# A new written order for a one-core kernel of linear attention and a highway layer: how x is turned, where the last columns are cut, and what fills TensorE at the start

## The chip, the core and the metric

The kernel runs on one core of a Trainium2 chip. A core has five engines with a queue each: TensorE (PE, matrix products, results in eight banks of PSUM), VectorE (DVE), ScalarE (ACT), GpSimd (POOL) and SyncE (SP, here the engine that issues nearly all DMA transfers). Each works through its own instructions in order and waits on semaphores for the others. The metric is the device time of one execution in microseconds (us), the median over several runs. Lower is better.

## The reference

The inputs are q, k and v of shape 4 x 8 x 768 x 64 (batch, heads, positions, head dimension), a decay `lam` per head, and a highway layer with two 512 x 512 matrices and a bias.

```python
for b in range(nb):                       # 12 blocks of 64 positions
    intra = einsum('bhic,bhjc->bhij', qb, kb) * Dmask      # Dmask[i,j] = lam**(i-j), i >= j
    intra = einsum('bhij,bhjd->bhid', intra, vb)
    inter = einsum('bhid,bhde->bhie', qb * lam_pow, kv_state)
    out[:, :, sl] = intra + inter
    kv_state = lam_block * kv_state + einsum('bhsd,bhse->bhde', kb * rev_pow, vb)
x = out.transpose(0, 2, 1, 3).reshape(3072, 512)
H = maximum(x @ w_h, 0);  T = sigmoid(x @ w_t + b_t)
return T * H + (1 - T) * x
```

## The kernel before

The work is cut into 12 steps n = 0 to 11: three for each of the four batches, of 256 positions each. A step holds two tiles b = 0, 1 of 128 positions, all eight heads in it, and the highway layer runs on the same tile of 128 x 512. Instead of a state that is scaled in each block, q is multiplied by lam to the position and v by its inverse, so that the state of a batch is a plain sum in PSUM (the bank `pair`, seen as `kv`).

The order in which everything is issued stands in a string, `PLAN`. It is a list of tokens that is executed from the left. Each token names an action, a step, mostly a tile or half, after `@` the engine and after `=` the PSUM banks (0 to 6). The compiler does not reorder, so each engine's queue is the sequence of its tokens. The tokens:

- `Lq`, `Lk`, `Lv` load half a step of q, k or v (256 KB each) on SyncE, or on ScalarE's queue with `@ACT`. `W` loads half of a weight matrix, `WC` casts a quarter of it to bf16.
- `CQ`, `CK`, `CV` make bf16 of q (times its power), k, and v (times its power); the last number is the half, 2 means both at once. `CQ` and `CV` run mostly on POOL.
- `TQ`, `TK` turn q and k on TensorE by products with the identity: in the form with a last number 0 in 64-row pieces (32 for both together), with 1 whole (16 for both). `EB` copies the result out of PSUM.
- `S`, and `SP` with the state sums `U` woven in, are the score products; `M` multiplies them by the mask on DVE; `KE` copies the state out; `I` are the products with the state, `A` those of the masked scores with v (the value products). `D` copies the finished x, which is turned (position along the free axis), to `xT`.
- `XT` turns x back on TensorE and `XE` copies it to `xr`. `XD` does the same by a DMA transpose from SyncE, without TensorE and without a copy. `xr` has three buffers, `xT` six.
- `PB` presets a bank with the bias, `F.n.b.w` multiplies the tile with a weight matrix (w = 0 for h, 1 for the gate t), `H` is relu minus x on DVE, `G` the sigmoid in place on ACT, `X` the product of both on DVE, `AD` the final sum (POOL mostly), `ST` the store. A further number p takes only the columns 256 p to 256 p + 255 of 512.
- `Z` are idle products: r times identity times zeros into a bank, which nothing reads. `ZT` does one into each bank, at the very start. `B` makes the bias row into 128 rows.

The loads have five buffers for each of q, k and v, the transfers eight completion semaphores, which the issues take in turn: an issue waits until the one eight places ahead has landed. Functions that matter: `turn` and `evac_x` (L375 to L393 of the kernel before), `block` (L405), `small` (L412), `spin` (L453), `open_banks` (L457).

Of the kernel before, what the change touches and what calls it, by code (L numbers as in the profile page):

```python
# [22 lines left out]
I.1.1=0 I.1.0=4 SP.1.1=6 CK.2.2@POOL D.0.1@ACT D.0.0@ACT M.1.0.0@DVE M.1.0.1@DVE W.1.0 TK.2.1=35 W.1.1 KE.1.1@ACT
WC.0.0.1@ACT WC.0.0.0@DVE Lq.3.1 Lq.3.0 WC.0.1.1@DVE WC.0.1.0@ACT CQ.2.2@POOL XT.0=2 A.1.1 A.1.0 D.1.1@DVE TQ.2.1
D.1.0@ACT F.0.0.0=6 XE.0@DVE EB.2.0@ACT XT.1=0 F.1.1.0=2 CV.2.2@POOL WC.1.1.0@POOL EB.2.1@DVE XE.1@DVE PB.0.1@ACT=4
WC.1.0.1@ACT PB.0.0@ACT=1 H.1.1@DVE WC.1.0.0@ACT F.0.1.0=5 F.1.0.0=0 H.0.0@DVE SP.2.0=362 H.0.1@DVE H.1.0@DVE Lk.3.0
Lk.3.1 M.2.1.1@DVE M.2.1.0@DVE M.2.0.0@DVE WC.1.1.1@ACT F.0.1.1 KE.2.0@ACT PB.1.1@ACT=0 G.0.1@ACT F.0.0.1 I.2.1=3
I.2.0=6 X.0.1@DVE SP.2.1=2 F.1.1.1 M.2.0.1@DVE CQ.3.2@POOL Lv.3.0 PB.1.0@ACT=5 AD.0.1@POOL TQ.3.0=24 Lv.3.1 G.0.0@ACT
CK.3.2@ACT Lq.4.0 Lq.4.1 TK.3.0 CV.3.2@POOL CQ.4.2@POOL X.0.0@DVE A.2.1 A.2.0 EB.3.1@ACT EB.3.0@DVE D.2.1@DVE
G.1.1@ACT D.2.0@ACT F.1.0.1 X.1.1@DVE SP.3.0=426 G.1.0@ACT KE.3.0@ACT Lk.4.0 Lk.4.1 Lv.4.0 XT.2=0 Lv.4.1 I.3.1=3  # L30
M.3.0.0@DVE M.3.1.1@DVE AD.1.1@POOL XE.2@ACT CK.4.2@ACT SP.3.1=1 F.2.1.0=6 M.3.0.1@DVE CV.4.2@POOL TQ.4.0=02 Lk.5.0
Lk.5.1 Lq.5.1 Lq.5.0 A.3.1=1 M.3.1.0@DVE AD.0.0@POOL A.3.0 TK.4.0 PB.2.1@ACT=4 D.3.1@ACT H.2.1@DVE D.3.0@DVE
EB.4.1@DVE X.1.0@DVE KE.3.1@ACT EB.4.0@ACT F.2.0.0=6 AD.1.0@POOL H.2.0@DVE XT.3=1 SP.4.0=023 F.2.1.1 KE.4.0@DVE
PB.2.0@ACT=5 XE.3@ACT I.4.1=6 I.4.0=1 M.4.1.1@DVE M.4.1.0@DVE M.4.0.0@DVE SP.4.1=2 Lv.5.1 CQ.5.2@POOL Lq.6.1 Lv.5.0
Lq.6.0 Lk.6.1 Lk.6.0 F.2.0.1 M.4.0.1@DVE Lv.6.1 Lv.6.0 CV.5.2@POOL G.2.1@ACT CK.5.2@ACT TK.5.0=30 X.2.1@DVE TQ.5.0
EB.5.1@DVE A.4.1 CQ.6.2@POOL A.4.0 KE.4.1@ACT G.2.0@ACT PB.3.1@ACT=4 CV.6.2@POOL Lq.7.0 Lk.7.0 D.4.0@ACT Lq.7.1
D.4.1@ACT EB.5.0@DVE Lk.7.1 F.3.1.0=2 SP.5.0=301 H.3.1@DVE F.3.1.1 CK.6.2@ACT M.5.1.1@DVE X.2.0@DVE TK.6.1=26 Lv.7.0
# [477 lines left out]
```

## Time and profile before

| what | us |
|---|---|
| median of three runs | 102.2 (102.17 to 103.01) |
| profiled execution | 102.22 |
| its span, first to last instruction | 100.5 |
| TensorE busy | 90.9 (90%) |
| VectorE busy | 81.1 (81%) |
| GpSimd busy | 74.5 (74%) |
| ScalarE busy | 72.0 (72%) |

DMA moved 28.61 MB, 285 GB/s in the mean. A product of TensorE is shown with a modelled end, so its busy time also holds short waits between products. The chain of waits is followed back from the last instruction: each piece is the work that released the next. In the timeline, what stands in square brackets is the idle time of that engine just before and what ended it.

### The profile page before, as it was taken

The page shows a single profiled execution, that of the slowest core. Times are in us where ns is not written, and L with a number is a line of the kernel's source. Part 1 is how long each engine was busy: PE and PEld are TensorE (multiplying, and loading weights), DVE is VectorE, ACT ScalarE, POOL GpSimd, SP SyncE. Part 2 cuts the span into 40 slices and gives each one's busy share as a digit, 9 for nine tenths or more (in the row PEclk, how much of TensorE's full clock was granted, in tenths as well). Part 3 has the DMA queues.
Part 4 walks back from the last instruction along what each step waited for, and adds up shares of the span by engine and source line. Part 5 has one row for each costly group of instructions (what it writes and reads, how often), then busy time and mean ns, then how long its engine had stood idle before and what let it go on. Part 6 is the DMA issues. An engine that isn't in the chain of part 4 may idle for free.

```text
span 100.5 us, 4427 instructions
## 1 busy us (share of the span) xinstructions
PE 90.9 (90%) x1891; PEld 54.0 (54%) x1891; DVE 81.1 (81%) x143; ACT 72.0 (72%) x123; POOL 74.5 (74%) x64
## 2 busy tenths in 40 slices
PE   4988999999998999999999999999999999999400
PEld 1314455873465666657656576666555565458200
DVE  4225386999987899999999979989998969996840
ACT  2436307989679899999799999887999867563400
...
GB/s 9 234 331 366 351 362 400 373 394 352 334 266 332 358 363 306 285 298 342 313 303 294 295 305 320 324 354 316 184 312 342 147 156 52 182 251 290 373 110 108
DMA packets 41222, 28.61 MB, mean 285 GB/s; under 512 B 6129, under 2 KB 37361, under 8 KB 41202
## 3 DMA queue, kind: packets, MB, share of 16 engines
...
q10 hardware_dynamic: 418, 0.27, 0.8%
...
HBM read 20.98 MB, written 6.29 MB: 271 GB/s over the span
## 4 chain that ended last, share of the span: by engine, by line
PE 74%; DVE 9%; ACT 5%; DMA 4%; POOL 2%; issue 1%; ACTq 0%; POOLq 0%; DVEq 0%
PE pb L409 40%; PE pb L296 8%; DVE m L349 6%; PE pb L367 5%; PE pb L271 5%; PE pb L357 4%; DMA qf<-in_q_dram 4%; PE pb L455 3%; PE pb L268 2%; PE kv L301 2%; POOL qb L243 2%; PE pb L383 2%; ACT kqT L110 2%; ACT pb L422 2%; DVE gxh L425 1%; PE pb L451 1%
## 5 line engine op out<-in xcount | busy, mean ns | idle before, releaser
L409 PE MATMUL pb<-w_b,xT 128*128 128x512 bf16 (+1 forms) x208 | 46.6, 364 | 0.5 <-ACT pb L422 0.4
L349 DVE TENSOR_TENSOR m<-pb,tri 128x512 bf16<-128x512 f32 x48 | 31.0, 682 | 4.3 <-PE pb L296 4.0
L428 POOL TENSOR_TENSOR o<-gx,xr 128x512 f32<-128x512 bf16 x22 | 25.2, 1154 | 10.3 <-DVE gx L425 8.3
L243 POOL TENSOR_TENSOR qb<-qf,pow_q 128x1024 bf16<-128x1024 f32 (+1 forms) x14 | 23.7, 1693 | 5.8 <-DMA qf<-in_q_dram 5.8
L409 PEld LDWEIGHTS <-xT 128*128 128x128 bf16 x208 | 18.2, 97 | 17.3 <-issue 0.9
L250 POOL TENSOR_TENSOR vs<-vf,pow_v 128x1024 bf16<-128x1024 f32 (+1 forms) x12 | 21.2, 1772 | 3.0 <-DMA vf<-in_v_dram 3.0
L422 ACT ACTIVATE pb<-pb 128x512 f32<-128x512 f32 (+1 forms) x26 | 14.1, 552 | 5.0 <-PE pb L409 3.8
L110 ACT ACTIVATE kqT<-pb 128x1024 bf16<-128x1024 bf16 x12 | 12.2, 1024 | 6.6 <-PE pb L268 4.2
L425 DVE TENSOR_TENSOR gx<-pb,hm 128x512 bf16<-128x512 f32 x22 | 15.0, 683 | 1.0 <-ACT pb L422 0.3
L417 DVE SCALAR_TENSOR_TENSOR hm<-pb,xr 128x512 bf16<-128x512 f32 x22 | 14.7, 683 | 0.8 <-PE pb L409 0.8
L296 PE MATMUL pb<-kqT 64*64 64x128 bf16 x384 | 14.7, 220 | 0.6 <-ACT xT L110 0.3
L403 ACT ACTIVATE pb<-bt_all 128x512 f32<-128x512 f32 x24 | 14.1, 602 | 0.9 <-DVE m L349 0.5
L296 PEld LDWEIGHTS <-kqT 64*64 64x64 bf16 x384 | 11.0, 105 | 3.9 <-ACT kqT L110 1.2
L110 ACT ACTIVATE xT<-pb 128x512 bf16<-128x512 f32 x19 | 10.9, 595 | 2.7 <-PE pb L367 2.6
L301 PE MATMUL kv<-vs,kb 64*64 64x64 bf16 x320 | 11.8, 193 | 0.0
L110 ACT ACTIVATE kb<-kf 128x1024 bf16<-128x1024 f32 (+1 forms) x10 | 10.1, 1011 | 1.7 <-DMA kf<-in_k_dram 1.7
L112 DVE COPY kqT<-pb 128x1024 bf16<-128x1024 bf16 x12 | 8.1, 686 | 2.4 <-PE pb L271 2.3
L301 PEld LDWEIGHTS <-kb 64*64 64x64 bf16 x320 | 9.8, 107 | 0.4 <-issue 0.4
L110 ACT ACTIVATE ss<-kv 128x256 bf16<-128x256 f32 x17 | 6.5, 385 | 2.4 <-PE pb L296 1.6
L367 PE MATMUL pb<-m,vs 64*64 64x128 bf16 x384 | 7.7, 218 | 0.2 <-DVE m L349 0.2
L455 PE MATMUL pb<-blank,id 128*128 128x512 bf16 x26 | 7.8, 439 | 0.0
L367 PEld LDWEIGHTS <-vs 64*64 64x64 bf16 x384 | 6.0, 106 | 2.6 <-issue 2.3
...
## 6 DMA issues: line engine op xcount, KB each, us to landing
...
```

The lines of the kernel that those rows point to most:

```text
L110: A.activation(dst, src, AF.Copy)
L243: ENG[eng].tensor_tensor(new(("qb", n), [128, 4, 4, D])[:, :, ys], in0=get("qf", n)[:, ys].rearrange("p y (i d) -> p i y d", i=4), in1=pow ...
L250: ENG[eng].tensor_tensor(new(("vs", n), [128, H, J, D])[:, hs], in0=get("vf", n)[:, hs].rearrange("p h (j d) -> p h j d", j=J), in1=pow_v[ ...
L296: T.matmul(get("s", n, e, hp // 2)[half(b), hp % 2, j, :], lhsT=keys(n, e, hp, j, b), rhs=queries(n, e, hp, b), start=first("s", n, e, hp ...
L301: T.matmul(kv[half(e), hp], lhsT=get("kb", n)[half(b), j, 2 * hp + e, :], rhs=get("vs", n)[half(b), 2 * hp + e, j, :], start=fresh, stop=T ...
L349: V.tensor_tensor(new(("m", n, e, u), [128, 2, J, C]), in0=get("s", n, e, u), in1=tri[:, None].to_broadcast([128, 2, J, C]), op=ALU.mult)
L367: T.matmul(get("o", n, b)[half(e), hp, :], lhsT=get("vs", n)[half(b), 2 * hp + e, j, :], rhs=get("m", n, e, u)[half(b), hp % 2, j, :], sta ...
L409: T.matmul(t, lhsT=get("xT", n, b)[:, kc, :], rhs=w_b[w][:, kc, cs], start=(w == 0 and kc == 0), stop=(kc == KC - 1), skip_group_check=boo ...
L417: V.scalar_tensor_tensor(small("hm", n, b, p), in0=get("h", n, b, p), scalar=0.0, in1=get("xr", n)[:, b, cols(p)], op0=ALU.max, op1=ALU.su ...
L422: A.activation(t, t, AF.Sigmoid)
L425: V.tensor_tensor(small("gx", n, b, p), in0=get("t", n, b)[:, cols(p)], in1=get("hm", n, b, p), op=ALU.mult)
L428: ENG[eng].tensor_tensor(small("o", n, b, p, F32), in0=get("gx", n, b, p), in1=get("xr", n)[:, b, cols(p)], op=ALU.add)
```

## The change

The string is replaced by another. What the actions compute stays the same, apart from the last tile (below). What differs, as far as the steps of the text need it:

- x of steps 0, 1 and 2 is turned with two banks: `XT.0=35` makes sixteen transposes of 64 rows instead of eight of 128, and the copies `XE.n.0` and `XE.n.1` take half each. Steps 3 to 6 and 11 use one bank, and steps 7 to 10 the DMA transpose. Before, steps 0 to 7 used one bank, and 8 to 11 the DMA.
- q and k are turned whole in steps 0, 1, 2, 3, 5 and 10. Before, in 1, 2 and 6.
- In the last tile the columns 256 to 511 are two pieces of 128 (p = 2 and 3). Of the last one the result is formed as relu(h) t + (x - t x) by `GS`, `GX`, `GW`, `HR` and `OT`, which existed unused.
- Idle products: 34 after the opening ones, of which there are eight. Before, 26 and seven. They stand at other places: 12 ahead of the first `TK`, then 4, 1, 8, 5 and 4, the last ahead of step 2's scores. `Y` and `spin_kv` are new and not called.
- Step 0's q products move from POOL to DVE. The loads stand in another order: k's second half on ScalarE's queue instead of a half of q, the first weight half ahead of step 2's loads.

The diff, with one line of the string before and one of the string after:

```diff
-Lq.0.1 Lq.0.0@ACT CQ.0.1@POOL CQ.0.0@POOL Lk.0.0 Lk.0.1 CK.0.0@DVE ZT Z.6=6 TQ.0.0=01 Lv.0.0 Lv.0.1 CK.0.1@ACT Lq.1.0
...
+Lq.0.0 Lk.0.1@ACT Lq.0.1 CQ.0.1@DVE CQ.0.0@DVE Lk.0.0 CK.0.0@DVE CK.0.1@ACT Lv.0.0 ZT Z.12=6 TK.0.1=01 TQ.0.1 Lv.0.1
...
-BUFS = dict(kf=5,qf=5,vf=5,kb=3,qb=3,vs=3,kqT=3,m=8,xT=6,xr=3,hm=4,gx=4,hmh=4,gxh=4,ss=4,o=12,oh=4)
+BUFS = dict(kf=5,qf=5,vf=5,kb=3,qb=3,vs=3,kqT=3,m=8,xT=6,xr=3,hm=4,gx=4,hmh=4,gxh=4,ss=4,o=12,oh=4,gsh=1,gwh=1,gvh=1,grh=1)
...
     def cols(p):
-        return slice(0, DM) if p is None else slice(256 * p, 256 * p + 256)
+        return slice(0, DM) if p is None else slice(256 * p, 256 * p + 256) if p < 2 else slice(128 * p, 128 * p + 128)
...
     def small(name, n, b, p, dtype=BF16):
         cs = cols(p)
-        return new((name, n, b, p), [C, cs.stop - cs.start], dtype, tag=name if p is None else name + "h")
+        w = cs.stop - cs.start
+        key = (name, n, b, p)
+        if key not in made:
+            made[key] = new(key, [C, max(w, DM // 2)], dtype, tag=name if p is None else name + "h")[:, 0:w]
+        return made[key]
...
+    def spin_kv(r):
+        for _ in range(r):
+            T.matmul(pair[:, 256:512], lhsT=id128, rhs=blank[:, 0:256], start=False, stop=True, skip_group_check=True)
+
     def open_banks():
-        for t in banks:
+        for t in [pair] + banks:
             T.matmul(t, lhsT=id128, rhs=blank, start=True, stop=True)
```

**VectorE at the start.** The queue before, from step 0's k cast on (`kf` is k as loaded, `kb` its cast, `qb` and `vs` q and v times their powers, `kqT` q and k turned, `ss` the state, `m` the masked scores; the numbers count tiles):

```order
L112 CAST kb_161<-kf_64 128x4x2x64
L112 COPY kqT_213<-pb_149 128x1024
L250 TENSOR_TENSOR vs_237<-vf_74,pow_v 128x512 x2
L112 CAST ss_263<-kv 128x256
L349 TENSOR_TENSOR m_311<-pb_153,tri 128x512
L112 CAST kb_307<-kf_65 128x4x2x64
```

The same place after:

```order
L244 TENSOR_TENSOR qb_157<-qf_69,pow_q 128x4x128 x2
L113 CAST kb_161<-kf_64 128x4x2x64
L251 TENSOR_TENSOR vs_202<-vf_74,pow_v 128x512 x2
L113 COPY kqT_207<-pb_148 128x8x2x64
L350 TENSOR_TENSOR m_252<-pb_148,tri 128x512
L350 TENSOR_TENSOR m_301<-pb_152,tri 128x512
```

The two q products stand ahead of the k cast, and v's products ahead of the copy of the turned k. The first state copy and step 1's k cast have gone to ScalarE.

**TensorE at the end.** The products behind step 11's value products, one row for each run of equal ones, without the weight loads between them (`w_b0` is the matrix of h, `w_b1` that of t; `xT4` and `xT5` belong to step 11). Before:

```order
L409 MATMUL pb6_154<-w_b1_146,xT2_554 128x512
L409 MATMUL pb3_151<-w_b0_145,xT2_554 128x512
L409 MATMUL pb1_149<-w_b0_145,xT3_564 128x512
L409 MATMUL pb5_153<-w_b1_146,xT3_564 128x512
L409 MATMUL pb3_151<-w_b0_145,xT5_782 128x256
L409 MATMUL pb2_150<-w_b0_145,xT5_782 128x256
L409 MATMUL pb0_148<-w_b1_146,xT5_782 128x256
L409 MATMUL pb1_149<-w_b0_145,xT4_779 128x256
L409 MATMUL pb4_152<-w_b1_146,xT4_779 128x256
L409 MATMUL pb2_150<-w_b0_145,xT4_779 128x256
```

After, behind two full blocks of step 10:

```order
L410 MATMUL pb4_152<-w_b1_146,xT5_748 128x128
L384 MATMUL pb1_149<-id128_106,xT4_738 128x128
L384 MATMUL pb1_149<-id128_106,xT5_748 128x128
L410 MATMUL pb5_153<-w_b0_145,xT0_375 128x512
L410 MATMUL pb6_154<-w_b1_146,xT0_375 128x512
L410 MATMUL pb1_149<-w_b0_145,xT5_748 128x128
L410 MATMUL pb0_148<-w_b0_145,xT4_738 128x256
L410 MATMUL pb3_151<-w_b1_146,xT4_738 128x256
L410 MATMUL pb5_153<-w_b0_145,xT5_748 128x256
L410 MATMUL pb4_152<-w_b1_146,xT5_748 128x256
L410 MATMUL pb1_149<-w_b0_145,xT4_738 128x256
```

A quarter of the last tile and the turning of step 11's x now stand ahead of two full blocks of step 9, and the two tiles' pieces alternate.

**SyncE at the end.** Before, from the last DMA transposes on (`o` and `oh` are results):

```order
L396 DMA_TRANSPOSE xr_855<-xT_779 128x4x128
L396 DMA_TRANSPOSE xr_855<-xT_782 128x4x128
L447 DMA out_dram<-o_85 128x512
L447 DMA out_dram<-o_84 128x512
L447 DMA out_dram<-o_82 128x512
L447 DMA out_dram<-o_86 128x512
L447 DMA out_dram<-o_87 128x512
L447 DMA out_dram<-o_88 128x512
L447 DMA out_dram<-oh_91 128x256
```

After:

```order
L397 DMA_TRANSPOSE xr_746<-xT_668 128x4x128
L452 DMA out_dram<-o_80 128x512
L452 DMA out_dram<-o_84 128x512
L452 DMA out_dram<-o_83 128x512
L452 DMA out_dram<-o_90 128x512
L452 DMA out_dram<-o_87 128x512
L452 DMA out_dram<-o_88 128x512
L452 DMA out_dram<-o_86 128x512
L452 DMA out_dram<-o_82 128x512
L452 DMA out_dram<-o_89 128x512
L452 DMA out_dram<-oh_91 128x128
```

The last transposes belong to step 10 instead of 11, and twelve full stores follow them instead of six.

More of the change, by code (lines that the diff above doesn't have):

```diff
@@ L23 @@
[L23 to L37, printed above, removed]
@@ new lines @@
+X.0.0@DVE XT.1=25 D.2.0@DVE F.1.1.1 Lq.6.0 Lq.6.1 XE.1.0@DVE D.2.1@DVE Lv.5.0 Lk.6.1 CK.3.2@ACT XE.1.1@ACT G.0.1@ACT
+G.1.1@ACT X.0.1@DVE F.1.1.0=1 H.1.1@DVE X.1.1@DVE TK.3.1=52 TQ.3.1 CV.3.2@POOL CK.4.2@ACT EB.3.1@ACT XT.2=60
+CQ.5.2@POOL TQ.4.0=31 TK.4.0 F.1.0.0=4 EB.3.0@DVE XE.2.1@DVE EB.4.1@ACT CK.5.2@ACT EB.4.0@DVE SP.3.0=205 H.1.0@DVE
+XE.2.0@DVE M.3.1.1@DVE KE.3.0@ACT F.2.0.0=3 M.3.0.0@DVE TQ.5.1=61 TK.5.1 I.3.1=0 AD.1.1@POOL M.3.1.0@DVE Lk.6.0
+PB.2.0@ACT=4 SP.3.1=5 F.2.0.1 EB.5.1@ACT KE.3.1@ACT M.3.0.1@DVE A.3.1=1 A.3.0 H.2.0@DVE EB.5.0@DVE CV.4.2@POOL
@@ new lines @@
+H.3.1@DVE F.3.1.1 KE.5.0@ACT M.5.1.0@DVE M.5.0.0@DVE M.5.1.1@DVE D.4.1@ACT SP.6.0=260 PB.4.1@ACT=5 M.6.1.1@DVE XT.4=1
+XE.4@ACT G.3.1@ACT Lk.8.1 Lq.9.1 Lv.7.0 Lq.8.1 Lk.10.1 M.6.0.0@DVE M.6.1.0@DVE CK.7.2@ACT F.4.1.1 Lv.8.1 Lv.10.1
+Lk.8.0 KE.6.0@ACT I.5.0=6 Lk.9.1 Lq.8.0 I.5.1=3 CV.7.2@POOL CQ.7.2@POOL SP.5.1=1 M.5.0.1@DVE F.4.0.0=0 A.5.1 A.5.0
+Lk.10.0 ST.0.1 Lq.10.0 Lv.10.0 Lq.10.1 Lv.8.0 X.3.1@DVE D.5.0@ACT I.6.1=4 AD.2.1@POOL AD.3.1@POOL CQ.8.2@POOL
+AD.3.0@POOL SP.6.1=1 H.4.0@DVE Lv.11.0 Lq.11.0 ST.3.1 Lq.11.1 D.5.1@DVE TK.7.0=20 M.6.0.1@DVE TQ.7.0 EB.7.1@DVE
@@ new lines @@
+AD.5.0@POOL F.6.0.0=5 TQ.10.1=60 TK.10.1 H.6.0@DVE EB.8.1@ACT D.7.1@ACT PB.6.1@ACT=2 EB.10.1@DVE Lk.11.0 ST.1.1
+D.7.0@ACT Lk.11.1 Lv.11.1 SP.8.0=145 EB.10.0@ACT F.6.1.0=3 M.8.1.1@DVE M.8.0.0@DVE M.8.1.0@DVE CK.9.2@ACT KE.8.0@ACT
+H.6.1@DVE F.6.1.1 TQ.9.0=60 XD.7.0 TK.9.0 EB.9.1@DVE G.6.1@ACT EB.9.0@ACT I.8.0=1 I.8.1=5 SP.8.1=3 M.8.0.1@DVE
+CK.11.2@ACT XD.7.1 X.6.1@DVE F.7.1.0=4 SP.9.0=603 A.8.1 A.8.0 F.7.0.0=2 H.7.1@DVE PB.7.0@ACT=4 F.7.0.1 D.8.1@ACT
+PB.6.0@ACT=5 D.8.0@ACT CQ.11.2@POOL AD.5.1@POOL ST.2.1 ST.1.0 M.9.0.0@DVE KE.9.0@DVE M.9.1.1@DVE CV.10.2@POOL
@@ new lines @@
+XE.11@DVE GX.11.1.3@POOL PB.11.0@ACT=3 X.10.0@DVE F.11.1.0.3=1 G.9.0@ACT H.9.0@DVE GW.11.1.3@POOL HR.11.1.3@DVE
+F.11.0.0.0=0 F.11.0.1.0 F.11.1.1.2 AD.10.0@POOL OT.11.1.3@POOL X.9.0@DVE AD.9.0@POOL H.11.0.0@DVE F.11.1.0.2=1
+G.11.0.0@ACT G.11.1.2@ACT F.11.1.0.0=5 F.11.1.1.0 G.11.1.0@ACT ST.10.0 ST.11.1.3 ST.9.1 H.11.1.2@DVE X.11.0.0@DVE
+F.11.0.0.1=1 AD.11.0.0@POOL F.11.0.1.1 X.11.1.2@DVE H.11.1.0@DVE ST.9.0 X.11.1.0@DVE G.11.0.1@ACT AD.11.1.2@POOL
+AD.11.1.0@POOL ST.11.0.0 ST.11.1.2 H.11.0.1@DVE X.11.0.1@DVE ST.11.1.0 AD.11.0.1@DVE ST.11.0.1
```

66 lines of the change are left out of this document (31 added, 35 removed).

## The prediction

> **What bounds the kernel now.** I read the windows of the whole run first, then the chain of waits from both ends, then the timeline of the start and SyncE's own rows at the end. The three long windows of the middle (columns: window, length, busy time and instructions of TensorE, weight loads, VectorE, ScalarE, GpSimd, then granted clock, DMA share, GB/s):
>
> ```profile
> 20.00:30.00 10.00, 9.81 (x173) 5.63 (x173) 9.49 (x17) 8.04 (x14) 5.87 (x5) 1.00 1.05 338
> 30.00:40.00 10.00, 9.44 (x276) 6.12 (x274) 8.88 (x15) 9.17 (x14) 9.63 (x7) 1.00 1.10 340
> 40.00:90.00 50.00, 49.96 (x1149) 30.02 (x1141) 46.03 (x75) 43.98 (x76) 42.17 (x30) 1.00 0.93 271
> ```
>
> From 20 to 90 us TensorE is idle for 70 - 69.21 = 0.8 us. VectorE is next: 64.4 of 70, so 5.6 us idle. The middle costs what TensorE has to do; an order alone can win 0.8 us there. The rest is before and after. The start, in the chain of waits (start, length, what) and then in the timeline:
>
> ```profile
> 1.24 4.25 DMA qf<-in_q_dram
> 5.65 2.24 POOL qb L243 x2
> 7.94 0.64 PE pb L271 x32
> 9.77 0.35 PE pb L296 x13
> 11.24 1.05 PE pb L451 x2
> 12.82 0.09 PE pb L296 x2
> 17.01 0.15 PE pb L296
> ```
> ```profile
> 1.43 3.17 PE L459 MATMUL pb<-blank,id 128*128 128x512 bf16 x7 [1.43 <-POOL id masks.py:199]
> 4.39 2.77 PE L455 MATMUL pb<-blank,id 128*128 128x512 bf16 x6
> 6.25 0.73 DVE L112 CAST kb<-kf 128x512 bf16<-128x512 f32 x1 [1.20 <-DMA kf<-in_k_dram]
> 7.07 0.63 ACT L110 ACTIVATE kb<-kf 128x512 bf16<-128x512 f32 x1 [1.73 <-DMA kf<-in_k_dram]
> 8.51 1.25 PE L455 MATMUL pb<-blank,id 128*128 128x512 bf16 x5
> 9.26 1.28 DVE L250 TENSOR_TENSOR vs<-vf,pow_v 128x512 bf16<-128x512 f32 x2
> 17.66 2.48 DVE L349 TENSOR_TENSOR m<-pb,tri 128x512 bf16<-128x512 f32 x4 [0.83 <-PE pb L296]
> ```
>
> The first transfers land at 5.6, 6.25 and 7.07 us, one per 0.75 us. The dummy products are 0.43 us apart up to 7.1 us and 0.22 us later. The end, first the chain, then SyncE's last issues:
>
> ```profile
> 86.14 0.57 PE pb L367 x32
> 86.72 5.76 PE pb L409 x36
> 92.47 0.06 issue
> ...
> 93.31 0.65 ACT pb L422 x2
> 94.00 0.61 PE pb L409 x4
> 94.70 0.38 ACT pb L422
> ...
> 96.35 0.42 DVE oh L428
> ```
> ```profile
> 94.90 0.33 SPq L447 DMA_DIRECT2D out_dram<-oh  x1
> 96.30 1.53 SPq L447 DMA_DIRECT2D out_dram<-oh  x1
> 97.92 0.38 SPq L447 DMA_DIRECT2D out_dram<-oh  x1
> ```
>
> TensorE rests about 1 us between 92.5 and 94.0, because the last half waits for a sigmoid in its own bank. The result is complete at 96.77, but the last store is issued only at 97.92: the issue ahead of it took 1.53 us instead of 0.33 to 0.38.
>
> The profiled execution took 102.22 us, 1.7 us over its span of 100.5; the median is 102.2, so the sum below stands for the median too. The edges of 1% are 101.2 and 103.2 us, about what a measurement of this kernel can tell from no change.
>
> **The change part by part.** The prices, from TensorE's pieces in the chain of waits and from the groups by shape:
>
> ```profile
> 30.14 1.02 ACT kqT L110
> 41.30 0.57 PE pb L271 x32
> 44.99 0.89 PE pb L268 x16
> 45.88 0.45 PE pb L383 x8
> L112 DVE COPY xr<-pb 128x1024 bf16<-128x1024 bf16 x4 | 2.7, 686 | 0.4 <-PE pb L383 0.4
> L112 DVE CAST xT<-pb 128x512 bf16<-128x512 f32 x5 | 3.4, 687 | 0.3 <-PE pb L367 0.2
> L112 DVE CAST ss<-kv 128x256 bf16<-128x256 f32 x3 | 1.3, 421 | 0.9 <-PE kv L301 0.7 <-PE pb L296 0.2
> L112 DVE CAST w_b<-w_f 128x512 bf16<-128x512 f32 x2 | 0.8, 417 | 0.0
> L417 DVE SCALAR_TENSOR_TENSOR hm<-pb,xr 128x512 bf16<-128x512 f32 x22 | 14.7, 683 | 0.8 <-PE pb L409 0.8
> L417 DVE SCALAR_TENSOR_TENSOR hmh<-pb,xr 128x256 bf16<-128x256 f32 x4 | 1.7, 418 | 0.8 <-DMA xr<-xT 0.8
> ```
>
> *TensorE's work.* Turning q and k in 64-row pieces costs 0.57 us a step, whole 0.89. Before, whole in 3 steps (1, 2, 6); after, in 6 (0, 1, 2, 3, 5, 10). Behind the start that is two more whole ones: +0.64. Turning x costs 0.45 by eight whole transposes; sixteen 64-row ones are half of the 0.57 row, 0.29. Steps 1 to 7 by TensorE cost 7 x 0.45 = 3.15; now 2 x 0.29 + 4 x 0.45 = 2.38 in steps 1 to 6, and 0.45 for step 11 falls in the end. Middle: +0.64 - 0.77 = **-0.1 us**.
>
> *The start.* Step 0's two q products (0.64 each as two of the kind take 1.28) move from GpSimd to VectorE, ahead of its k cast. They begin when the third transfer has landed, 6.25, end 1.28 later at 7.53, and the cast (0.75) at 8.3. On TensorE the 20 dummy products take 0.43 each to 7.1 and 0.22 afterwards: to 8.6. Turning whole: 9.5; ScalarE's copy as before 1.0: 10.5; four dummies, the states and one dummy more: scores at 11.0 instead of 9.77. What follows no longer waits for the bias product (1.05), moved behind: the stretch before ended at 12.9, now 12.5. Then VectorE's four masks and one state copy (11.4 to 14.7) hold the last value product; turning q and copying take until 16.4, the bias product on TensorE until 16.75, and step 1's scores start at 16.8 instead of 17.0. Behind them VectorE needs 1.9 for three masks, 0.42 + 0.42 and two copies (1.3): 21.5, step 2's scores 0.6: the first product with the weights at 22.3, where before it was 21.39. Scores of 0.6 us are done earlier by then, a value product of 0.5 is owed. Like for like 0.8 us later: **+0.8**. TensorE's own pieces from 8.6 on add up to 21.8, so not under +0.3; a transfer one place (0.75) later: +1.5.
>
> The Trainium skill (TensorE: Matmul & The Clock Gate, Part 1) has the full clock come about 3.4 us after sustained work begins, in a free-running window. The rows above show 5.7 us, from 1.43 to 7.1. By the page's figure the 20 dummies would end near 7.5, the cast at 8.3 would gate, and the start would be +0.5 instead of +0.8, an estimate.
>
> *VectorE's work.* Behind the start it gets three state copies (1.26), two x copies (1.37), one weight cast less (-0.42), and four full copies of xr become three full and three half ones (-0.69 + 3 x 0.42): +2.8 us of work. Its 5.6 us of idle time can take all of it (0) or, since its queue is in order and TensorE has no slack, none (+2.8). I take **+0.5**, near the idle row since that is twice the work; below, the 0.8 us that TensorE idles could go too.
>
> *The end.* From the end of step 11's value products: before, 86.72 to 96.77, 10.05 us. Now TensorE has four full blocks (0.87 each, at 0.216 a product), one turn of x (0.45), four quarter blocks (0.22) and six half ones (0.45; of the 36 products in 5.76 us, 16 are full and leave 0.115 for each of 20 halves): 7.5 us, with no wait that I find, since the pieces of both tiles alternate and each sigmoid is done before its bank is written again. Then a sigmoid of 0.38, a gate of 0.42 behind a relu that ends 0.4 later, the sum 0.42: 9.1. **-0.95**; up to 0 if the alternation fails. A 128-wide piece costs 0.29 us on VectorE (683 to 418 for half the width leaves 0.153 fixed), so cutting is not free, but it lies beside products. The skill (VectorE: DVE Perf Modes, errata) warns that many small tiles pay a fixed cost each; the two rows agree.
>
> *Stores and transposes by DMA.* Step 11's transposes leave SyncE's end, step 7's come in where none waits. But stores are late: behind the last transpose stand 12 of 256 KB and five small ones instead of 6 and 4. SyncE's issue time and the DMA rate there, for the last 16 us:
>
> ```profile
> L447 SPq DMA_DIRECT2D out_dram<-o x9: 332/430/538, 86.1 to 93.9; - x9
> GB/s 173 1 93 214 21 266 405 405 400 404 243 172 1 176 152 10 389 405 410 400 405 410 410 410 256 404 105 269 274 26 23 15 15 246 236 190 0 0 0 0
> ```
>
> At 405 GB/s a store takes 0.65 us, all of them some 8.6, with SyncE's 0.43 apiece beside that. Step 10's transposes have their input a step earlier, so I take them to be issued when step 11's value products end; then the stores are out 0.5 us before the last sum is ready at 9.1, hidden. Each us that the transposes come later than 0.5 after that point delays the end by one. *The last store.* Whether one issue takes 1.5 us again the trace cannot tell: one of four did. I take the three: **-1.1**, the other end 0.
>
> Sum: +0.8 - 0.1 + 0.5 - 0.95 - 1.1 = -0.85: span 99.65, with 1.7 **101.4 us**, 0.8% under before.
>
> **The rivals.**
> *A, the order pays.* VectorE's work fits into its idle time and TensorE's 0.8 us of waits go: -0.85 - 0.5 - 0.8 = -2.15, 100.1 us. For it: the middle is full in both, and the dummy products fill just those stretches in which I find waits. Against: VectorE at 92% has more to do.
> *B, VectorE becomes the bound in the middle.* It decides once its queue runs behind TensorE by more than a step, from some 1 us of the 2.8. All 2.8 appear: -0.85 - 0.5 + 2.8 = +1.45, 103.7 us, slower. For it: 9.49 busy of 10 in the window from 20. Against: two of the added copies are taken from ScalarE where that was late.
> *C, a long issue again, or late stores.* +1.1 to the forecast: 102.5.
> *D, the halves gain nothing,* since 64-row transposes come while TensorE has dummies to do: three steps, 0.5 us at most; it only moves the sum inside the range.
>
> **How the numbers follow.** Forecast 0.27, C 0.16 (both within 1%), A 0.38, B 0.19. A lies under 101.2, and a tenth of the forecast's cases with it: faster 0.41, within 1% 0.40, slower 0.19. The range reaches from A with a start of +0.5 (99.8) to B (103.7).
>
> **What would show it.** The first product with the weights near 22.3 us: the start is right; before 21.6, wrong. TensorE idle from 24 to 85 us: under 1 us speaks for the forecast or A, 2 us and more, ended by VectorE, for B. From step 11's last value product to the last sum 9.1 us without a rest of TensorE. The last four store issues under 0.6 us each; if one takes 1.5, C. A store that is issued over 0.5 us after its sum would make the end wrong.

## The result and the profile after

The changed kernel takes 106.37 us in the median (105.46 to 107.51, four runs) against 102.61 us for the old one on the same chip (102.17 to 103.73): a ratio of 1.035, 95% interval 1.024 to 1.046. Slower, where 0.8% less was forecast. Ratios here and below leave disturbed runs out, medians do not; a median is compared with that of the old kernel in the same session (101.7 to 102.6).

The profiled execution took 106.40 us with a span of 104.7, 4.2 more than before. Four stretches share it (the first product with weights, the end of step 11's value products and the last sum are the marks):

| stretch | before | after | difference | forecast |
|---|---|---|---|---|
| start to the first product with weights | 21.2 | 23.4 | +2.1 | +0.8, like for like |
| from there to step 11's last value product | 65.5 | 69.1 | +3.6 | +0.4 |
| from there to the last sum | 10.06 | 9.60 | -0.46 | -0.95 |
| last sum to the end of the span | 3.74 | 2.66 | -1.08 | -1.1 |

The old kernel's 21.2 is where its first such product starts (21.22); the prediction's 21.39 is where the chain of waits comes to it. In the middle TensorE's rests grew from 0.6 to 3.8 us, its work from 64.9 to 65.3. The windows of after (columns as in the prediction's first fence):

```profile
20.00:30.00 10.00, 10.00 (x224) 6.21 (x225) 7.87 (x14) 7.69 (x15) 5.62 (x6) 1.00 1.08 351
30.00:40.00 10.00, 9.37 (x244) 6.34 (x242) 9.49 (x18) 7.89 (x13) 9.89 (x6) 1.00 1.06 320
40.00:90.00 50.00, 46.83 (x1064) 27.67 (x1061) 43.68 (x73) 40.64 (x69) 40.86 (x29) 1.00 0.85 238
60.00:70.00 10.00, 9.17 (x204) 5.58 (x204) 7.84 (x14) 8.31 (x14) 8.31 (x6) 1.00 1.02 315
70.00:80.00 10.00, 7.73 (x209) 4.76 (x201) 7.43 (x14) 7.28 (x12) 10.00 (x7) 1.00 0.66 149
```

VectorE is less busy from 40 to 90 us than before (43.68 against 46.03), so it did not become the bound. Two other columns stand out: the DMA share is 1.0 up to 70 us, and GpSimd is busy for all of the ten us from 70. What TensorE waited for between 15 and 90 us, and GpSimd between 55 and 70 (sum, times, longest):

```profile
PE pb L410 <- ACT pb L404: 1.7, 1, 1.7
PE pb L272 <- ACT kb L111: 1.1, 2, 0.6
PE pb L269 <- ACT kb L111: 0.9, 1, 0.9
PE pb L269 <- POOL qb L244: 0.8, 1, 0.8
```
```profile
POOL vs L251 <- DMA vf<-in_v_dram: 2.4, 1, 2.4
```

The 0.9 us is step 2's `TK` at 19.1; the 0.8 is step 10's `TQ` at 65.5; 0.5 of the second row is step 9's `TK` at 70.2; the other 0.6 of that row is step 4's `TK` at 32.6; the 1.7 is step 7's third block, its first for the gate, at 74.9. The last one, followed back in the chain of waits (start, length, what), and then SyncE's issues before it in the timeline:

```profile
63.10 4.42 DMA qf<-in_q_dram
...
67.67 1.91 POOL qb L244
...
69.85 5.23 DMA xr<-xT
...
75.17 0.70 DVE hm L422
...
75.96 0.60 ACT pb L404
```
```profile
52.23 0.61 SPq L149 DMA_DIRECT2D kf<-in_k_dram  x1
...
53.77 0.61 SPq L147 DMA_DIRECT2D qf<-in_q_dram  x1
54.42 1.41 SPq L149 DMA_DIRECT2D vf<-in_v_dram  x1
55.88 1.31 SPq L147 DMA_DIRECT2D qf<-in_q_dram  x1
57.23 1.15 SPq L149 DMA_DIRECT2D vf<-in_v_dram  x2
...
67.69 0.63 SPq L149 DMA_DIRECT2D vf<-in_v_dram  x1
68.43 2.62 SPq L397 DMA_TRANSPOSE xr<-xT  x2
```

Step 7's second transpose is issued at 69.85, behind the last load, and lands 5.23 us later (the median before was 2.6); relu, then the preset of the bank, then TensorE wait for it. The rows at 52 to 56 us are step 10's k, q, v, q. Only then, at 57.23, comes the second half of step 8's v. GpSimd waits 2.4 us for it, with step 10's q behind it in its queue.

The end: TensorE's part was 7.52 us, as forecast (7.5); from its last product to the last sum it took 2.1 us instead of the forecast's 1.6, since relu and gate of two pieces share VectorE:

```profile
94.94 4.16 PE pb L410 x36
...
99.17 0.38 ACT pb L427
...
99.58 0.29 DVE gxh L430
99.87 0.34 DVE hmh L422
...
100.23 0.42 DVE gxh L430
100.66 0.34 DVE hmh L422
...
101.61 0.43 DVE oh L433
```

### The profile page after: what moved, and what is told of

Read it like the earlier page. It is cut to its first block, busy times and chain, and to the rows that moved or that the text cites. A ratio compares the mean times of both kernels' runs of the same rounds, so it can differ in the third digit from the quotient of the medians.

```text
span 104.7 us, 4427 instructions
## 1 busy us (share of the span) xinstructions
PE 93.8 (90%) x1884; PEld 55.8 (53%) x1884; DVE 82.8 (79%) x150; ACT 71.6 (68%) x122; POOL 73.0 (70%) x66
## 4 chain that ended last, share of the span: by engine, by line
PE 33%; SPq 27%; DMA 21%; ACT 7%; POOL 4%; DVE 3%; issue 3%; DVEq 0%; ACTq 0%; POOLq 0%
PE pb L410 22%; SPq L149 15%; DMA qf<-in_q_dram 8%; SPq L147 7%; DMA kf<-in_k_dram 5%; DMA xr<-xT 5%; SPq L230 4%; POOL qb L244 4%; DMA out_dram<-o 3%; PE pb L297 2%; PE pb L358 2%; ACT pb L404 2%; PE pb L368 2%; ACT xT L111 2%; SPq L452 1%
## 5 line engine op out<-in xcount | busy, mean ns | idle before, releaser
L410 PE MATMUL pb<-w_b,xT 128*128 128x512 bf16 (+2 forms) x216 | 46.5, 356 | 1.8 <-ACT pb L404 1.7
L244 POOL TENSOR_TENSOR qb<-qf,pow_q 128x1024 bf16<-128x1024 f32 (+1 forms) x12 | 21.1, 1759 | 15.4 <-DMA qf<-in_q_dram 15.4
L410 PEld LDWEIGHTS <-xT 128*128 128x128 bf16 x216 | 18.5, 98 | 18.5 <-issue 2.2
L427 ACT ACTIVATE pb<-pb 128x512 f32<-128x512 f32 (+2 forms) x26 | 13.9, 543 | 4.5 <-PE pb L410 4.4
L111 ACT ACTIVATE kb<-kf 128x1024 bf16<-128x1024 f32 (+1 forms) x13 | 12.3, 955 | 4.5 <-DMA kf<-in_k_dram 4.5
L297 PE MATMUL pb<-kqT 64*64 64x128 bf16 x384 | 14.2, 220 | 0.0
L111 ACT ACTIVATE xT<-pb 128x512 bf16<-128x512 f32 x17 | 9.9, 597 | 4.2 <-PE pb L368 4.2
L460 PE MATMUL pb<-blank,id 128*128 128x512 bf16 x34 | 9.3, 414 | 0.0
L111 ACT ACTIVATE ss<-kv 128x256 bf16<-128x256 f32 x14 | 5.3, 381 | 2.6 <-PE kv L302 2.6
```

Source lines behind the costliest of these rows:

```text
L111: A.activation(dst, src, AF.Copy)
L244: ENG[eng].tensor_tensor(new(("qb", n), [128, 4, 4, D])[:, :, ys], in0=get("qf", n)[:, ys].rearrange("p y (i d) -> p i y d", i=4), in1=pow ...
L297: T.matmul(get("s", n, e, hp // 2)[half(b), hp % 2, j, :], lhsT=keys(n, e, hp, j, b), rhs=queries(n, e, hp, b), start=first("s", n, e, hp ...
L410: T.matmul(t, lhsT=get("xT", n, b)[:, kc, :], rhs=w_b[w][:, kc, cs], start=(w == 0 and kc == 0), stop=(kc == KC - 1), skip_group_check=boo ...
```

## The experiments

Theory A of the first runs: the new order of the loads makes the rests (in the start, step 2's k behind the weights; in the middle, step 10 loaded ahead of 8 and 9), and step 7's transposes by DMA add one. The rivals stand with each run. "First product" is short for the first product with weights.

### The order of the first loads

```diff
-Lq.2.1 Lq.1.1 Lk.1.0 Lq.1.0 Lk.1.1 Lv.1.0 Lv.1.1 W.0.0 Lk.2.1 Lq.2.0 Lk.2.0 Lv.2.0 Lv.2.1 W.0.1
+Lq.1.1 Lk.1.0 Lq.1.0 Lk.1.1 Lv.1.0 Lv.1.1 Lk.2.1 Lk.2.0 Lq.2.1 Lq.2.0 W.0.0 W.0.1 Lv.2.0 Lv.2.1
-WC.0.0.1@ACT CK.2.2@ACT
+CK.2.2@ACT WC.0.0.1@ACT
```

> The changed kernel with the first loads in the old kernel's order (step 1's, then step 2's k and q, then the weights), and ScalarE's cast of step 2's k ahead of its cast of the first weights; nothing else moves. Theory A (the order of the loads costs the start): the first transpose of step 2's k, which started at 20.0 us after 0.88 us of rest, starts near 18.9; the first product with weights comes at 22.3 instead of 23.4; the time falls from 106.4 to about 105.2. Rival B (the loads as a whole set the pace later): the start moves up as in A, but the rests at 65 to 76 us grow by the same amount, and the time stays at 106.4 +- 0.3. Rival C (the unused products or the 64-row tiles hold the start): the first product with weights stays at 23.4, time 106.4.

105.98 us (103.34 to 108.07), ratio 1.017 (1.003 to 1.031). Step 2's first transpose started at 18.5 instead of 20.0, as theory A had it, but the first product came at 23.8, later than before. TensorE's wait from 18 to 26 us, and GpSimd's rows:

```profile
PE kv L302 <- POOL vs L251: 1.4, 1, 1.4
```
```profile
17.20 1.90 POOL L244 TENSOR_TENSOR qb<-qf,pow_q 128x1024 bf16<-128x1024 f32 x1 [2.24 <-DMA qf<-in_q_dram]
21.23 1.90 POOL L251 TENSOR_TENSOR vs<-vf,pow_v 128x1024 bf16<-128x1024 f32 x1 [2.12 <-DMA vf<-in_v_dram]
```

Now v was late, and step 2's scores and states, which the new order puts ahead of the first product, wait for it. So the start has more than one load to wait for. The shortest run, 103.34, is 1.6 us under the shortest of all ten runs of the changed kernel (104.92), the longest is as long; this alone doesn't tell more.

### Step 7 on TensorE, the late loads in order, and both

Step 7 on TensorE:

```diff
-XD.7.0 ... XD.7.1
+XT.7=4 XE.7@DVE
```

> The changed kernel with step 7's x turned by TensorE (8 transposes into one bank, evicted by VectorE) instead of by two DMA transposes; nothing else moves. Theory A (the DMA transpose behind the last loads is what step 7 waits for): the rest of 1.72 us at 74.9 us goes, 0.7 us of transposes come back, some of them inside the rest of 0.48 us at 70.2; time 106.4 to about 105.2. Rival B (VectorE is the bound in the middle, as the prediction's rival had it): VectorE's eviction of about 0.8 us comes on top and the time rises to 106.5 to 107.2. Rival C (the rest at 74.9 only stands in for the late loads of step 11): the rest moves to step 11's transposes at about 77 us, time 106.4 to 107.

The late loads in the order of the steps (casts, transposes and evictions of steps 9 and 10 exchange their names, so that 9 is made first):

```diff
-Lk.8.1 Lq.9.1 Lv.7.0 Lq.8.1 Lk.10.1 Lv.8.1 Lv.10.1 Lk.8.0 Lk.9.1 Lq.8.0 Lk.10.0 Lq.10.0 Lv.10.0 Lq.10.1 Lv.8.0 ...
+Lv.7.0 Lk.8.1 Lk.8.0 Lq.8.1 Lq.8.0 Lv.8.1 Lv.8.0 Lk.9.1 Lk.9.0 Lq.9.1 Lq.9.0 Lv.9.1 Lv.9.0 Lq.10.1 Lq.10.0 ...
```

> The changed kernel with the loads from step 8 on in the order of the steps (8, 9, 10, 11), and the casts, transposes and evictions of steps 9 and 10 renamed to match, so that step 9's are made first; the number and the places of the instructions stay. Theory A (the order of the loads costs the middle): the rests of 0.83 us at 65.5 and 0.48 us at 70.2 go, TensorE's rest between 60 and 72 us under 0.3; time 106.4 to about 105.1, and lower if the step 7's transposes by DMA, which stand behind the last loads, come in earlier too. Rival B (only the DMA transposes of step 7 matter): the rests at 65 and 70 go, the rest at 74.9 grows to about 3 us, time 106.4 +- 0.4. Rival C (the DMA engines are the limit, in whatever order): the rests stay, time 106.4.

Both, with the changed kernel's own start, and both with the first loads of the run above:

> The changed kernel with the late loads in the order of the steps and step 7's x turned by TensorE, but with its own start. Theory A (both middle edits are needed, and the start's load order is worth nothing since the supply of loads decides there): 103.5 to 104.4, as with the three edits together, first product with weights at 22.8 to 23.4, TensorE's rests between 40 and 85 us under 0.3 us in all. Rival B (the start's load order did carry part of the gain of the three edits): 105.0 or more, with a start as late as the changed kernel's.

> The three edits of the other runs together: first loads in the old order, late loads in the order of the steps, step 7's x turned by TensorE. Theory A (three separate costs that add): 106.4 - 1.2 - 1.3 - 1.2 = 102.7, and TensorE's rests of over 0.05 us after 20 us sum to under 1.3 us instead of 3.7. Rival B (they hide behind each other; something else of the change holds the middle): over 104.5, with VectorE or ScalarE named at the rests that are left. Rival C (the prediction's likeliest case comes back): 101.4 to 102.2, under the old kernel's time.

| late loads | step 7 by DMA | step 7 on TensorE |
|---|---|---|
| as changed | 106.37; ratio 1.035 (1.024 to 1.046) | 107.65; 1.052 (1.040 to 1.064) |
| in order | 106.58; 1.030 (1.016 to 1.045) | 104.10; 1.014 (1.004 to 1.024) |

With the other first loads as well: 104.12, 1.020 (1.012 to 1.028). Neither edit is seen to gain alone, both together take 2.3 us off. The profiles say in part why. TensorE's longest wait from 40 to 90 us, and GpSimd's from 55 to 70, with step 7 on TensorE (109.1 us in the profiled run, the longest of the four):

```profile
PE pb L269 <- POOL qb L244: 2.8, 1, 2.8
```
```profile
POOL vs L251 <- DMA vf<-in_v_dram: 3.4, 1, 3.4
```

and TensorE's with the late loads in order (105.65 us), where GpSimd waits for no load at all in that stretch:

```profile
PE pb L410 <- ACT pb L404: 2.4, 1, 2.4
```

Each edit removes its own rest and leaves the other, longer than before. For the rest at step 7's blocks (2.4 us instead of 1.7) that can follow from the edit. The rest at step 10's `TQ` stands ahead of the edited tokens, so turning step 7 on TensorE can't have lengthened it to 2.8; in two profiles of the unaltered kernel it is 0.8 and 2.5 us (below), so it differs from run to run. Both long rests also cost more than their length, since TensorE ran at half its clock for the 3.41 us behind them. With the late loads in order (columns as in the first fence, the clock is the number ahead of the DMA share):

```profile
75.17:78.58 3.41, 3.08 (x68) 2.10 (x68) 2.75 (x6) 2.94 (x5) 1.09 (x1) 0.50 0.52 139
```

Half of the 3.1 us of work there, some 1.5 us, is the price, an estimate. In the run with both, TensorE has no wait over 0.5 us from 40 to 90 us, and the windows show little rest. Its four runs still scatter (102.54 to 104.75); with the first loads in order too they lie between 103.59 and 104.43.

```profile
65.00:70.00 5.00, 4.89 (x97) 3.21 (x89) 3.80 (x7) 4.55 (x8) 5.00 (x4) 1.00 1.09 357
70.00:75.00 5.00, 4.89 (x138) 3.06 (x134) 5.00 (x10) 3.71 (x6) 5.00 (x4) 1.00 0.10 36
75.00:80.00 5.00, 4.79 (x147) 3.15 (x149) 4.96 (x10) 4.35 (x9) 3.17 (x3) 1.00 0.72 120
```

None of the last expectation's three times came: 104.1 is over A's 102.7, under B's 104.5, and rival C, the forecast's 101.4 to 102.2, did not come back.

### The transposes taken away

```diff
-XD.7.0 ... XD.7.1
...
-get("xr", n)
+get("xr", 6 if n == 7 else n)
```

> The changed kernel without step 7's two DMA transposes and with nothing in their place (step 7 takes step 6's turned x, so its values are not the reference's). Theory A (on the old kernel two transposes cost 3.3 us since no other transfer moves while they run, so they are dear wherever they stand): the rest of 1.72 us at 74.9 us goes, the rest of the transfers comes out earlier; time 104.0 to 104.8. Rival B (the loads of steps 9 and 10 alone make the middle): the rests at 65 and 70 us stay or grow, since they come before the transposes, and the time stays over 105.5.

107.13 us (105.82 to 107.79), ratio 1.048 (1.039 to 1.057): rival B. In the profiled run, its longest, TensorE waited for step 10's q for 3.8 us, again ahead of the edited place. So taking the transposes away alone isn't seen to gain; the late loads come ahead of them.

### Less to load

```diff
-            e.dma_start(out=new((x + "f", n), [128, H, J * D], F32)[:, hs], in_=src.rearrange("h (p j) d -> p h (j d)", j=J))
+            t, src = new((x + "f", n), [128, H, J * D], F32)[:, hs], src.rearrange("h (p j) d -> p h (j d)", j=J)
+            if x == "v" and n >= 5:
+                t, src = t[:, 0:2], src[:, 0:2]
+            e.dma_start(out=t, in_=src)
```

> The changed kernel with only half of v loaded from step 5 on (two of the four heads of each transfer; the other half of each tile keeps what an earlier step left, so these values are not the reference's): 14 transfers of 256 KB become 128 KB, 1.8 MB of 28.6 less, about 5.7 us of the DMA engines' time at 320 GB/s. The instructions and their order stay. Theory A (the 16 DMA engines are busy to about 67 us, so a load that stands too late in the order lands late, and that makes the rests of the middle): TensorE's rests between 60 and 78 us fall from 3.1 us to under 1, and the time from 106.4 to 103.0-104.0. Rival B (the order of TensorE's and VectorE's own work makes the rests): they stay over 2.5 us, time 105.8 to 106.5.

103.40 us (103.32 to 104.28), ratio 1.015 (1.006 to 1.024): theory A. With the same instructions in the same order, 6% fewer bytes take 3.0 us off by the medians, 2.0% by the ratios. Of the rests between 60 and 78 us one is left:

```profile
PE pb L413 <- ACT pb L407: 0.8, 1, 0.8
```

That step 8's v is the one load that matters did not hold, however. Its loads early alone, and with step 7 on TensorE:

```diff
-Lq.8.1 Lk.10.1 Lv.8.1 Lv.10.1 ... Lq.10.1 Lv.8.0
+Lq.8.1 Lv.8.1 Lv.8.0 Lk.10.1 Lv.10.1 ... Lq.10.1
```

> The changed kernel with the two loads of step 8's v put ahead of step 10's and 9's loads; nothing else. Theory A (GpSimd waits for step 8's second half of v, and step 10's q stands behind it on GpSimd): GpSimd's wait for v between 58 and 64 us falls from 2.4 to under 0.5, TensorE's rest at step 10's transposes from 0.8 (up to 3.8 in other runs) to under 0.2; the rest at 74.9 may grow by part of that; time 105.0 to 106.0. Rival B (some other load of step 10 is as late): the rest at 65 stays over 0.7, time as before.

> The changed kernel with the two loads of step 8's v early, as in the run with them alone (106.8), and step 7's x turned by TensorE. Theory A (step 8's v is the load that holds the middle, and the DMA transposes take its place when it is mended): 104.0 to 104.8, as with all late loads in order. Rival B (step 9's loads, which stand last, hold it as much): the rests at step 9's transposes, 0.3 and 0.7 us at 68 to 69, stay or grow; 105.0 to 106.5.

106.81 us, ratio 1.039 (1.033 to 1.045), and 106.32, 1.038 (1.028 to 1.048). GpSimd's wait for v and the rest at step 10's `TQ` went, but step 9's loads stand last and take over (0.7 us and 0.3 us at step 9's `TK` and `TQ`), then step 7's transposes (1.8), or, with step 7 on TensorE, step 8's: VectorE waits 1.5 us for them around 80 us, TensorE 1.5 at 83. Of the orders tried, only all late loads in order, with step 7 on TensorE, free the middle.

The changed kernel once more, for its scatter:

> The changed kernel itself, unaltered, five rounds. Theory A (the rest at step 10's transposes depends on when step 8's second half of v lands, which differs from run to run by 1 to 3 us): the median stays at 106.0 to 107.0 with single runs from 104.5 to 108, more scatter than the old kernel's; in the profiled run the rests at step 10's transposes and at step 7's blocks come again, with other lengths than 0.83 and 1.72 us. Rival B (the profiled run of before was typical to a tenth): all runs within 106.4 +- 0.5.

106.34 us, 104.92 to 107.92 in six runs, ratio 1.032 (1.024 to 1.039). In the profiled run, 106.89 us, step 10's `TQ` waited 2.5 us instead of 0.8, and from 40 to 90 us TensorE had no other wait over 0.5. Step 7's rest of 1.72 us did not come again, other than theory A had it. But the clock fell here too, right behind the wait:

```profile
PE pb L267 <- POOL qb L242: 2.5, 1, 2.5
```
```profile
68.74:72.14 3.40, 3.18 (x51) 1.89 (x49) 2.38 (x4) 1.99 (x3) 3.40 (x3) 0.50 1.12 341
```

### Two more transposes on the old kernel

```diff
-XT.7=2 ... XE.7@DVE
+XD.7.0 XD.7.1
```

> The old kernel with step 7's x turned by two DMA transposes, put right behind the step's second copy into xT, instead of by TensorE and VectorE; nothing else moves. Theory A (the transpose by DMA is dear in the changed kernel only because it is issued late, 5.2 us before it lands, right ahead of the relu that needs it): here it is issued at about 66 us, some 6 us ahead of its relu, nothing waits for it, and 0.45 us of TensorE's and 0.8 of VectorE's work go: the old time, or up to 0.5 us less. Rival B (transposing by DMA in the middle costs by itself, by holding the transfers behind it): the last loads land later and TensorE rests at step 11's transposes, the old time + 0.7 to + 2.

> The old kernel with step 7's x turned by DMA as in the earlier run (105.6), but with the last load, half of step 11's v, issued ahead of the two transposes instead of four transposes behind. Theory A (no other transfer moves during a transpose, so the load behind them came 4.5 us later, and step 8's transposes 4 us later): the rest of 1.6 us at step 11's scores goes, the rest of 1.5 us at step 8's gate and value blocks stays; time 103.6 to 104.4. Rival B (the time is lost in the transposes that queue behind one another alone): 105 or more. Rival C (all of it was that load): 102.0 to 102.6.

The first took 105.59 us, ratio 1.034 (1.024 to 1.044): rival B, though with 3.3 us above its 0.7 to 2, for taking work off TensorE. With the last load ahead of the transposes it was 102.62 us, ratio 1.005 (1.001 to 1.008), nearly all of it back: rival C. SyncE's rows in the dear one:

```profile
66.20 5.29 SPq L396 DMA_TRANSPOSE xr<-xT  x2
...
72.22 3.20 SPq L396 DMA_TRANSPOSE xr<-xT  x2
...
76.10 0.43 SPq L148 DMA_DIRECT2D vf<-in_v_dram  x1
```

The load of step 11's v is issued at 76.10 instead of 71.57, and step 8's pair at 72.22 instead of 68.28. TensorE's and VectorE's waits from 60 to 90 us:

```profile
PE kv L301 <- POOL vs L250: 1.6, 1, 1.6
PE pb L409 <- DVE hm L417: 1.5, 1, 1.5
```
```profile
DVE hm L417 <- DMA xr<-xT: 3.0, 2, 2.4
```

With the load ahead the first row is gone, and the second still shows 1.3 us in the profiled run (103.34 us, above the median). While step 7's pair is in flight the DMA engines move little besides; their rate in the dear run in 40 slices of 2.6 us:

```profile
GB/s 8 248 344 361 355 373 384 383 384 347 264 309 326 318 261 304 287 269 311 320 308 329 340 359 336 346 320 42 202 173 349 299 252 10 101 327 173 406 215 93
```

The 42 is the slice from 70 to 72.5 us, between the issue of step 7's second transpose and of step 8's first.

### The start

First two blocks with weights ahead of step 2, as in the old kernel (edit of the run with three edits):

```diff
-... WC.0.1.1@POOL ... Z.4=3 SP.2.0=203 M.2.1.0@DVE F.0.1.0=6 F.0.0.0=2
+... WC.0.1.1@DVE ... F.0.1.0=6 F.0.0.0=1 SP.2.0=203 M.2.1.0@DVE
```

> The kernel of the three edits together (104.1), with the first two blocks of products with weights put ahead of step 2's scores and states, as the old kernel has them, the three unused products there left out, and one cast of the weights moved from GpSimd to VectorE and ahead of step 2's v. Theory A (the start is late since step 2's scores and states, which need three more loads, v's, stand ahead of the first product with weights): the first product with weights moves from 23.7 to between 21.0 and 22.0, TensorE's rest of 1.05 us at 22 goes, and the time falls by 1.0 to 2.0, to 102.1 to 103.1. Rival B (the supply of loads decides, so that the rest appears later, at steps 3 to 5): the first product is early but the rests at 30 to 40 us grow by as much; 103.6 to 104.3. Rival C (the work of 64-row tiles and of VectorE holds the start): no product with weights before 23.

107.03 us (104.88 to 107.32); there is no ratio for it. In the profiled run, the longest of the four, the first product came at 22.3 us, after 1.5 us of waiting, and two more rests of 1.1 and 1.3 us followed. From 27.6 us TensorE ran at half its clock:

```profile
24.17:27.57 3.40, 1.53 (x81) 1.25 (x80) 2.95 (x5) 0.38 (x1) 1.72 (x2) 1.00 1.12 347
27.58:34.40 6.82, 6.25 (x73) 3.27 (x74) 2.73 (x6) 4.64 (x10) 5.63 (x4) 0.50 0.95 291
```

```profile
PE pb L410 <- DVE m L350: 1.5, 1, 1.5
PE pb L358 <- DVE m L350: 1.1, 1, 1.1
```

The second fence has TensorE's waits from 18 to 26 us: it waited for VectorE's masks; the 1.3 us came after, for ScalarE's copy of the state. None of the three as stated: 22.3 us is later than A's 21.0 to 22.0 and earlier than C's 23, though the waits name VectorE, as C has it. What the edit costs without the loss of clock is open: the shortest run, 104.88 us, shows a mean granted clock of 0.994, the profiled one 0.955.

Then the loads in the order in which they are asked for, and the casts of the weights put behind, both with the middle's two edits, and the start's edits alone:

```diff
-Lq.2.1 Lq.1.1 ... Lv.1.1 W.0.0 Lk.2.1 Lq.2.0 Lk.2.0 Lv.2.0 Lv.2.1 W.0.1
+Lq.1.1 ... Lv.1.1 Lk.2.1 Lk.2.0 Lq.2.1 Lq.2.0 Lv.2.0 Lv.2.1 W.0.0 W.0.1
```
```diff
-WC.0.0.1@ACT CK.2.2@ACT ... WC.0.0.0@DVE Z.5=6 ... XE.0.0@ACT KE.1.1@ACT WC.0.1.0@ACT ... Z.4=3
+CK.2.2@ACT ... Z.5=6 ... XE.0.0@ACT WC.0.0.1@ACT WC.0.0.0@ACT WC.0.1.0@ACT KE.1.1@ACT ... Z.2=3
```

> The same two middle edits, and the first loads in the order in which TensorE's order asks for them: step 1's, step 2's k, q and v, then the weights. Theory A (the order of the first loads is what the start lacks): step 2's first transpose near 18.6, its scores near 21.3, the first product with weights at 21.9 to 22.4, time 102.6 to 103.4. Rival B (the bytes decide: 5.5 MB must have landed before the first product with weights in this order, against 4 MB in the old kernel's, and at 300 to 370 GB/s the last of them land at the same time in any order): the weights become the late ones, first product with weights at 22.8 to 23.8, time 103.5 to 104.4.

> The changed kernel with both middle edits, the first loads in the order in which they are asked for (103.6 so far), and the first three casts of the weights put on ScalarE behind step 0's two evictions, so that nothing that waits for a weight stands ahead of step 2; the unused products there are 2 instead of 4. Theory A (the casts that wait for the weights hold VectorE and ScalarE, and with them step 2's evictions): TensorE's rest of 1.19 us at 19.8 goes, step 2's scores start at 21.1 to 21.6 instead of 22.7, the first product with weights at 21.8 to 22.3 instead of 23.4, time 102.0 to 102.7. Rival B (the bytes hold the start): the weights land at 20 to 21 and are cast by 22.5 at the earliest, first product at 22.8 or later, time 103.2 to 103.8.

> The changed kernel with the edits of its start alone (first loads as they are asked for, casts of the weights behind, 2 unused products for 4); middle and end as they are. Theory A (start and middle are separate costs): first product with weights 1.0 to 1.5 us earlier than 23.4, the rests of the middle as before, time 104.9 to 105.6. Rival B (the middle is held by the loads, which come no sooner): the start is earlier, the rests at 65 to 76 grow by as much, time 106.0 to 107.

103.56 us (ratio 1.017, 1.010 to 1.023), 103.63 (1.016, 1.011 to 1.021) and 106.23 (single runs from 104.33 to 107.51, over the times of both its theories, so it decides between neither; the two shortest are 3% above the old kernel). First products at 23.4, 23.2 and 22.7 us. In the first two step 2's v is cast by 20.9 and 21.5 us instead of 22.3, so the order did what it should; what TensorE waited for instead, in the first and in the second:

```profile
PE pb L358 <- ACT xr L111: 1.2, 1, 1.2
```
```profile
PE kv L302 <- ACT ss L111: 0.6, 1, 0.6
```

that is ScalarE's copies of x (behind a cast that waited for the weights), then its copy of the state (behind the three casts). k, v, the masks, the copies of x, the state: each edit showed another wait, and the first product stayed between 22.3 and 23.8. That is about where it lies without any edit of the start: 22.7 to 23.4 in the ten profiles with the changed kernel's own start, against 21.2 to 21.4 in four with the old one. In the first two rival B's times came; that the bytes as such are the limit was not shown, since each time an engine's queue stood between.

### The end

The last 256 columns in one piece on the changed kernel, and the old kernel with alternating halves, uncut:

```diff
-F.11.1.1.3 ... GS GX GW HR OT ... F.11.1.0.3=1 ... F.11.1.1.2 ... F.11.1.0.2=1 ...
+F.11.1.1.1 ... F.11.1.0.1=1 ...
```

> The changed kernel with the last tile's last 256 columns in one piece again: the early quarter, with its sigmoid, three products and sum on the other path, is gone, and the late quarter is 256 columns wide. Theory A (the cut is worth what the prediction's term for the end says, about half of the 0.95 us): from the end of step 11's value products to the last sum 9.6 us becomes 10.0 to 10.2, the time 106.4 to 106.9. Rival B (the end is held by the alternation of blocks on TensorE alone, the cut gains nothing): 9.5 to 9.7, time 106.4.

```diff
-F.11.0.1.1 ... F.11.1.0.1=1 ... F.11.1.1.1 ... F.11.1.0.0=2 F.11.1.1.0
+F.11.1.0.1=1 ... F.11.1.1.1 ... F.11.1.0.0=2 F.11.0.1.1 ... F.11.1.1.0
```

> The old kernel with the halves of the last tile's two sub-tiles in alternating order at the end (one gate block moved between the last two value and gate blocks, sums spread over GpSimd and VectorE to match), uncut. Theory A (the rest of 0.41 us and the bunched VectorE work at the end go, which is all that the changed kernel gained there): from the end of step 11's value products to the last sum 10.06 becomes 9.2 to 9.6, time 0.4 to 0.9 us under the old kernel's. Rival B (the gain needs step 11's x turned by TensorE or the quarter pieces): 9.9 to 10.1, the old time.

Uncut, the stretch to the last sum is 9.65 us instead of 9.60 (time 107.04 us, ratio 1.039, 1.024 to 1.055): the cut gains nothing. On the old kernel the alternation alone brings 10.06 to 9.60, all that the changed kernel gained there. In the whole time it is not to be seen: 102.01 us, ratio 0.999 (0.994 to 1.004).

## Why the prediction was wrong

**"The middle costs what TensorE has to do."** This premise failed. The fence behind it shows a DMA share of 1.05 and 1.10 as well; I read the engines' columns only, and the third row's 0.93 averages 40 us at 0.98 to 1.04 and a last ten at 0.59. So the DMA engines were a second bound, and the old order, with its loads nearly in the order of the steps, met it with 0.6 us of rests; for the old kernel that is read from the share alone. The sum had no term for loads that come late, though the diff moves them. Of the 3.8 us of rests after, 1.9 end by such loads (step 4's k, step 10's q behind step 8's v, step 9's k) and 1.7 by step 7's transposes. The bound is shown by the run with half of v (3.0 us back by the medians) and the order by the runs with the late loads in order and step 7 on TensorE: four such kernels have medians of 103.6 to 104.1 us, ten measurements of the changed kernel with at most one of the two edits and all bytes 106.0 to 107.7. A fifth with both, 107.0, ran at half its clock from 27.6 to 34.4 us in its profile.

**"Step 7's come in where none waits."** Failed. They stand right behind the last load and land in 5.2 us, and relu, a bank and TensorE wait 1.7 us. That this is a cost of its own shows in the lower row of the table (106.58 against 104.10), though the intervals of the two ratios overlap; on the old kernel the same two transposes cost 3.3 us with a load behind them and, by the ratio, about 0.5 without.

**The start, +0.8.** The mechanism, queues that hold one another, was right up to step 1's scores (forecast 16.8, measured 16.9). The part behind them failed: it adds VectorE's pieces up to 21.5 and puts the wait for step 2's k at nothing (only its upper end, +1.5, allows a transfer one place later), though the new order has half a weight matrix, two transfers' worth, ahead of it. ScalarE waited 1.5 us for that k and cast it from 18.85 us on, so step 2's `TK` began at 20.0, after 0.9 us of rest, and the first product came at 23.4 instead of 22.3. That the late k alone made it late isn't shown: with k ahead of the weights `TK` began at 18.5, and the product came at 23.8, behind v. No edit of mine brought it under 22.3, and what bounds the start stays open.

**TensorE's work, -0.1, and VectorE's, +0.5.** TensorE's busy time in the stretch rose by 0.4, where its own term was -0.1; that the two terms sum to 0.4 is chance, and VectorE was the limit of none of the rests. Rival B forecast the right sign by the wrong mechanism: the test that I set for it, two us and more of rest "ended by VectorE", tells it apart, since the rests end by loads, GpSimd and DMA transposes.

**The end, -0.95.** -0.46. TensorE's 7.5 was right and ran without a rest; "a gate behind a relu that ends 0.4 later" left out that VectorE has two pieces' gates and relus to do there, 2.1 us instead of 1.6. The rest of "about 1 us" in the old end, which the term was to win, is 0.41 us in TensorE's own rows. Rival A's price for the order as a whole (100.1) is out with the middle.

**The last store, -1.1.** -1.08, and none of the last four issues over 0.6 us. But it is not all the change's: the three variants of the old kernel show 3.03 to 3.04 us from last sum to end. So 0.7 of it was the long issue in the one profile, which did not come again in these, and 0.4 the new order's. That the stores stayed hidden was closer than the prediction has it: twelve of 256 KB and 512 KB in five small ones are 9.1 us at 405 GB/s, not 8.6, which leaves none of the 0.5 us to spare. Where the middle was mended, two of four profiles (first loads in the old order, and step 2's v ahead of the weights) show the last store issued 0.6 and 0.7 us after its sum, and 3.3 and 3.4 us from last sum to end instead of 2.7.
